# Attention, then an MLP, on one core: another hand-planned order, three split loads, eleven conversions moved off GpSimd

## The chip, the core and the metric

The kernel runs on one core of a Trainium2 chip. Its engines work side by side: TensorE (PE in the profile, PEld for its weight loads), VectorE (DVE), ScalarE (ACT), GpSimd (POOL) and SyncE (SP), which here only issues DMAs. Each engine takes its instructions in the order in which they were put on its queue, and waits at the first one whose inputs are not there. The metric is the device time of one execution in microseconds (us), the median of three runs for the kernel before. A profile is one such execution, recorded instruction by instruction.

## The reference: what is computed

```python
def _attn_ref(q, k, v, g_q, g_k):
    def rmsnorm(x, g):
        rms = np.sqrt(np.mean(x * x, axis=-1, keepdims=True) + 1e-06)
        return x / rms * g
    q_n, k_n = (rmsnorm(q, g_q), rmsnorm(k, g_k))
    scale = 1.0 / np.sqrt(q.shape[-1])
    scores = scale * np.matmul(q_n, k_n.transpose(0, 1, 3, 2))
    attn = softmax(scores)            # row maximum taken off, row sum + 1e-09
    return np.matmul(attn, v)

def _moe_ref(x, w_in, w_out):
    h = x @ w_in
    relu6 = np.clip(h + 3.0, 0.0, 6.0)
    g = h * relu6 / 6.0
    return g @ w_out
```

q, k and v are float32 of shape (batch 8, heads 12, sequence 448, width 64). The attention output, heads side by side, is x with 3584 rows and 768 columns. w_in is 768 x 2048 and w_out 2048 x 768. The result is 3584 x 768 in float32.

## The kernel before

Two heads make a pair; there are six pairs per batch element and 48 in all. A pair's q, k and v are loaded by SP in 256 KB each, with rows spread over 112 partitions and four rows (t = 0 to 3) to a partition. A pair then passes through these steps, named as in the kernel's plan:

- `ld`: a load (line 420). `sq` and `sqh`: squares of q or k, whole or half (L362 on ACT, L364 on POOL). `red2`, `red15`, `redh`: their sums over 64 elements, on DVE (L449, L483). `ln` and `ex`: the inverse root by logarithm and exponential, on ACT (L425, L428). `sc` and `sch`: q or k times it, in bfloat16 (L367; on POOL, a few on DVE).
- `tr` and `trh`: transposes on PE (L537) for the early pairs, with copies `cq`, `ck`, `cqh` out of PSUM (L348 to L358); `dt`: a transposing DMA for the later pairs (L556), after which `kt` multiplies in the gain (L564, L566).
- `s`: scores (L589, L612), two heads at once, each on 64 of PE's rows. `e`: their exponential on ACT (L595, L617). `cv`: v converted to bfloat16 beside a column of ones (L346 on DVE, L348 on ACT, L352 on POOL). `av`, `avh`: exponentials times v, which gives the row sums too (L634, L675). `rd` and `xn`: division by the row sum, on DVE. `xt` and `cx`, or the transposing DMA `dx` (L701): x in transposed form.
- `h1`, `h3`: products with w_in (L748, L767), two steps of three matmuls per group in the main part. `relu` on ACT (L726) and `gate` on DVE (L729) make g. `y384`: products with w_out, 384 columns wide, in four quarter steps of four matmuls (L789). `cy` copies them out, and `st` stores them.
- `w_in` and `w_out`: the weights, in four pieces each, issued by POOL (L820, L825).

The first batch element goes through a stage of its own in two half sequences, so that PE has products with w_in early; the main part then runs attention of one batch element beside the MLP of the one before it. The last 60 us hold MLP work alone.

What sets the order is a plan. All steps are first added to a list by `plan.add`, which numbers them and finds each step's predecessors from what it reads and writes. `Plan.emit` then issues them in the order of the list ORDER, a permutation of the 2386 numbers. `em` ties each instruction to the one issued before it on the same engine, so that ORDER alone decides every engine's order. Steps that more than one engine can do carry a list of engines; the table WAY gives, by number, which is taken, and the first one if the number isn't there:

```python
plan.add("cv", [POOL, ACT, DVE], f_v, [vr], [wr])
...
for i in order:
    kind, engines, fn, preds = self.ops[i]
    fn(engines[WAY.get(i, 0)])
```

A step is named here by its kind and its number: cv589 is step 589, a conversion. The numbers are the same before and after. The functions that the diff touches:

Of the kernel before, what the change touches and what calls it, by code (L numbers as in the profile page):

```python
# [204 lines left out]
def kernel(  # L205
# [11 lines left out]
    nc = tc.nc  # L217
# [4 lines left out]
    NP = B * NPAIR  # L222
# [107 lines left out]
    for t in T_r:  # L330
        nc.vector.memset(t[:, S2:], 0.0)
    for t in eT_r:
        nc.vector.memset(t[:, :, S2:], 0.0)

    NPT = 13
    NXB = 2
    YA = 3
    NSP = 2
    NW0 = 8
    NW1 = 22  # L340

    plan = Plan()
# [65 lines left out]
    def load(P, parts=(0, 1, 2)):  # L408
        b, j = divmod(P, NPAIR)
        hs = slice(2 * j, 2 * j + 2)  # L410
        for i in parts:
            src = (q, k, v)[i]
# [544 lines left out]
```

## Time and profile before

| what | value |
|---|---|
| three runs | 425.29, 425.38 (median), 426.16 us |
| the profiled execution | 425.55 us, of which 423.80 us are the span from first to last instruction |
| granted TensorE clock, mean | 0.998 |
| busy share of the span | PE 98%, ACT 68%, PEld 57%, DVE 53%, POOL 42% |
| DMA | 67.77 MB, mean 160 GB/s |

How to read it: a busy PE is not a PE at its peak, since matmuls overlap and their ends are modelled; the distance from one start to the next tells what one costs. A line of the timeline gives start, length, engine, source line, operation, output<-inputs, and how many were merged; in brackets stands how long the engine was idle before and what ended that. A line of the chain of waits gives start, length and what it was. Groups give a count, the busy time and the mean of one in ns, then the idle time before them and what ended it.

### The profile page before, as it was taken

What the parts mean: (1) busy time and instruction counts of PE and PEld (TensorE: products, weight loads), DVE (VectorE), ACT (ScalarE), POOL (GpSimd) and SP (SyncE); (2) the same over time, 40 slices, a digit from 0 to 9 for tenths busy, and PEclk for the clock granted to TensorE, in tenths of its full rate; (3) what the DMA queues carried; (4) which work ended last, traced back from release to release, by engine and by line L of the source; (5) the groups of instructions that cost most, each with busy time, mean ns of one, the idle gap of its engine ahead of it and who ended that gap; (6) DMA issues with size and microseconds to landing.
All of it is one profiled execution on the core that took longest, in us unless ns stands there. A gap on an engine that the chain in (4) does not pass through costs nothing.

```text
span 423.8 us, 9991 instructions
## 1 busy us (share of the span) xinstructions
PE 414.8 (98%) x3960; PEld 243.0 (57%) x3960; DVE 225.8 (53%) x453; ACT 287.1 (68%) x523; POOL 178.1 (42%) x206
## 2 busy tenths in 40 slices
PE   7999999989999999999999999999999999999996
PEld 3566877645555555555555555555555555555564
DVE  5988774769775476565445455543453433232310
ACT  6999988789987768787767867666846662133101
POOL 3999685678774462593035655333030200000000
PEclk9999999999999999999999999999999999999999
DMA  7999999999869958595768469273144202200323
GB/s 249 292 282 220 244 216 170 274 267 274 207 155 267 249 129 226 172 197 144 198 154 239 110 159 215 79 184 77 40 106 112 57 26 60 43 7 0 109 68 118
DMA packets 98931, 67.77 MB, mean 160 GB/s; under 512 B 53156, under 2 KB 95428, under 8 KB 98884
## 3 DMA queue, kind: packets, MB, share of 16 engines
q1 hardware_dynamic: 93248, 60.50, 54.6%
q0 software_dynamic: 5248, 6.29, 9.0%
q8 instruction: 31, 0.51, 0.5%
q10 hardware_dynamic: 388, 0.34, 0.3%
q14 instruction: 16, 0.13, 0.1%
HBM read 50.23 MB, written 11.01 MB: 145 GB/s over the span
## 4 chain that ended last, share of the span: by engine, by line
PE 84%; DMA 6%; ACT 4%; issue 1%; DVE 1%; SPq 1%; POOL 1%; DVEq 0%; POOLq 0%; ACTq 0%
PE M L767 28%; PE M L789 27%; PE X L675 9%; PE S L589 5%; PE S L789 5%; PE X L589 3%; PE M L748 3%; DMA qk<-in_q_dram 3%; ACT eT L617 3%; DMA w_in_sb<-in_moe_w_in_dram 2%; DMA vf<-in_v_dram 1%; PE X L767 1%; PE S L767 1%; POOL qks L367 1%; PE X L789 1%
## 5 line engine op out<-in xcount | busy, mean ns | idle before, releaser
L367 POOL TENSOR_TENSOR qks<-qk,rs 112x512 bf16<-112x512 f32 (+1 forms) x88 | 88.9, 1024 | 119.5 <-ACT rs L428 94.8
L789 PE MATMUL M<-w_out_sb,gT 128*128 128x384 bf16 x752 | 138.0, 326 | 0.0
L767 PE MATMUL M<-xT,w_in_sb 128*128 128x448 bf16 x618 | 134.0, 353 | 0.0
L789 PEld LDWEIGHTS <-gT 128*128 128x128 bf16 x912 | 84.2, 98 | 58.3 <-issue 7.3
L729 DVE SCALAR_TENSOR_TENSOR gT<-ts,M 128x448 bf16<-128x448 f32 x119 | 73.3, 616 | 74.5 <-ACT ts L726 74.3
L595 ACT ACTIVATE eT<-S 112x896 bf16<-112x896 f32 x112 | 99.7, 916 | 6.9 <-PE X L675 3.6
L726 ACT ACTIVATE ts<-M 128x448 f32<-128x448 f32 x119 | 64.9, 546 | 46.5 <-PE M L767 39.4
L767 PEld LDWEIGHTS <-w_in_sb 128*128 128x128 bf16 x672 | 60.3, 98 | 58.2 <-issue 11.9
L364 POOL TENSOR_TENSOR sq<-qk 112x512 f32<-112x512 f32 (+1 forms) x59 | 59.1, 1012 | 24.1 <-DMA qk<-in_q_dram 9.6
L595 ACT ACTIVATE eT<-X 112x896 bf16<-112x896 f32 x56 | 51.3, 917 | 20.2 <-PE X L589 19.2
L675 PEld LDWEIGHTS <-eT 112*128 112x128 bf16 x1344 | 52.3, 97 | 15.1 <-DVE va L346 1.5
L675 PE MATMUL X<-va,eT 112*128 112x65 bf16 x1344 | 55.3, 193 | 1.4 <-DVE va L346 1.1
L449 DVE TENSOR_REDUCE ssq<-sq 112x16 f32<-112x1024 f32 x42 | 50.7, 1212 | 7.1 <-ACT sq L362 3.8
L589 PE MATMUL S<-T 64*128 64x448 bf16 x224 | 34.1, 353 | 0.1
L350 DVE COPY y<-M 128x384 f32<-128x384 f32 x23 | 12.8, 557 | 39.1 <-PE M L789 39.1
L694 DVE TENSOR_TENSOR xn<-X,rd 112x512 bf16<-112x512 f32 x42 | 28.9, 689 | 2.1 <-DMA xT<-xn 1.3
L691 DVE RECIPROCAL rd<-X 112x8 f32<-112x8 f32 x42 | 8.7, 207 | 38.2 <-PE X L675 35.4
L589 PEld LDWEIGHTS <-T 64*128 64x128 bf16 x336 | 12.3, 94 | 24.0 <-issue 18.8
L362 ACT ACTIVATE sq<-qk 112x512 f32<-112x512 f32 (+1 forms) x38 | 22.2, 595 | 5.6 <-DMA qk<-in_q_dram 3.4
L348 ACT COPY y<-M 128x384 f32<-128x384 f32 x24 | 11.5, 480 | 19.0 <-PE M L789 18.7
L748 PE MATMUL M<-xT,w_in_sb 128*128 128x224 bf16 x192 | 23.1, 259 | 0.2 <-DMA w_in_sb<-in_moe_w_in_dram 0.2
L789 PE MATMUL S<-w_out_sb,gT 128*128 128x384 bf16 (+1 forms) x128 | 22.3, 316 | 0.0
(88 smaller groups left out, 303.1 us busy)
## 6 DMA issues: line engine op xcount, KB each, us to landing
qk<-in_k_dram SPq DMA_DIRECT2D x45, 256.0 KB, 4.2
qk<-in_q_dram SPq DMA_DIRECT2D x45, 256.0 KB, 4.0
vf<-in_v_dram SPq DMA_DIRECT2D x45, 256.0 KB, 4.3
w_in_sb<-in_moe_w_in_dram POOLq DMA_DIRECT2D x4, 768.0 KB, 8.5
w_out_sb<-in_moe_w_out_dram POOLq DMA_DIRECT2D x4, 768.0 KB, 9.2
out_dram<-y SPq DMA_DIRECT2D x7, 336.0 KB, 3.9
out_dram<-y SPq DMA_DIRECT2D x8, 288.0 KB, 3.5
out_dram<-y SPq DMA_DIRECT2D x8, 240.0 KB, 2.7
```

What stands on the lines that cost most here:

```text
L364: em(nc.gpsimd.tensor_tensor(out=out, in0=in_, in1=in_, op=A_MULT))
L367: em((nc.vector if e == DVE else nc.gpsimd).tensor_tensor(out=out, in0=in_, in1=by.unsqueeze(3).to_broadcast(list(in_.shape)), op=A_MULT))
L449: em(nc.vector.tensor_reduce(out=ssq[:].rearrange("p i n -> p (i n)"), in_=sq[:].rearrange("p i (n d) -> p (i n) d", d=D), axis=AX_X, op=A ...
L589: em(nc.tensor.matmul(out=ps[:, a, 0:S], lhsT=qkT[r, S + t * TP:S + t * TP + 128], rhs=qkT[r, 0:S], start=True, stop=True))
L595: em(nc.scalar.activation(out=eT[:, t, 0:S2].rearrange("p (a s) -> p a s", a=2), in_=ps[0:TP, :, 0:S], func=EXP, bias=0.0, scale=1.0))
L675: em(nc.tensor.matmul(out=X_ps[:, a, i * E1:(i + 1) * E1], lhsT=eT[:, t, c:c + 128], rhs=va[:, a, t, :], start=(t == 0 and i == 0), stop=( ...
L694: em(nc.vector.tensor_tensor(out=xn[:].rearrange("p i a d -> p a i d"), in0=view()[:, :, :, 0:D], in1=rd[:].unsqueeze(3).to_broadcast([TP, ...
L726: em(nc.scalar.activation(out=ts[:], in_=ps()[:, 0:S], func=RELU, bias=0.5, scale=1.0 / 6.0))
L729: em(nc.vector.scalar_tensor_tensor(out=out, in0=shape(ts[:]), scalar=1.0, in1=shape(ps()[:, 0:S]), op0=A_MIN, op1=A_MULT))
L748: em(nc.tensor.matmul(out=ps()[:, f * SH:(f + 1) * SH], lhsT=w_in_sb[:, kt, f0:f0 + 128], rhs=xT[:, kt, z * SH:(z + 1) * SH], start=(kt == ...
L767: em(nc.tensor.matmul(out=ps()[:, 0:S], lhsT=w_in_sb[:, kt, f * 128:(f + 1) * 128], rhs=xT[:, kt, :], start=(kt == 0), stop=(kt == NKT - 1)))
L789: em(nc.tensor.matmul(out=ps()[:, 0:nc0], lhsT=gT[:, f, i * 128:(i + 1) * 128], rhs=w_out_sb[:, f, c0:c0 + nc0], start=(f == 0), stop=(f = ...
```

## The change

The kernel after has the same 2386 steps with the same predecessors. Three things differ.

ORDER is another permutation. On PE, the number of instructions of every kind is the same; their sequence differs from the first few microseconds on. The runs of score steps, where PE goes from work on all its rows to work on half of them and back, have 178 edges in place of 180.

WAY has other entries. By kind and engine, before and after: `cv` POOL 26 and 15, DVE 17 and 21, ACT 5 and 12; `sqh` POOL 6 and 4, ACT 6 and 8; `sc` of the first six pairs DVE 4 and 1, POOL 2 and 5; `ck` DVE 9 and 11, ACT 4 and 2; `cq` DVE 5 and 7, ACT 2 and 0; `cqh` DVE 11 and 12, ACT 1 and 0; `cx` DVE 4 and 5, ACT 2 and 1; `kt` DVE 22 and 21, ACT 13 and 14; `cy384` DVE 27 and 29, ACT 28 and 26. `sq`, `sch` and `cxh` keep their numbers per engine.

The loads of v for the last three pairs (NSL = 3) go out as two DMAs of one head each.

```diff
 WAY = {
-    53: 1, 61: 1, 63: 2, 67: 1, 68: 1, 69: 1, 76: 1, 80: 1, 83: 1, 95: 1, 99: 1, 101: 2, 121: 1, 122: 1,
...
+    53: 1, 54: 1, 61: 1, 63: 2, 68: 1, 69: 1, 83: 1, 84: 1, 90: 2, 95: 1, 101: 1, 121: 1, 122: 1, 128: 2,
...
 ORDER = [
-    9, 20, 8, 21, 22, 10, 23, 11, 24, 25, 13, 28, 26, 14, 27, 53, 16, 31, 55, 32, 17, 33, 54, 212, 12, 34,
...
 ]
...
     NPT = 13
     NXB = 2
+    NSL = 3
...
-            def fn(_, dst=dst, src=src, np=np):
+            split = i == 2 and P >= NP - NSL
+
+            def fn(_, dst=dst, src=src, np=np, split=split):
                 rows = src[b, hs].rearrange("h (p t) d -> p h (t d)", t=T)
                 rows = bass.AP(rows.tensor, rows.offset, [[rows.ap[0][0], np]] + [list(d) for d in rows.ap[1:]])
-                em(nc.sync.dma_start(out=dst, in_=rows))
+                for h in ((0, 1) if split else (slice(0, 2),)):
+                    em(nc.sync.dma_start(out=dst[:, h], in_=rows[:, h]))
```

Of the new ORDER, the stretch that matters most for SP reads, loads and transposes alone: dt663, ld262, ld590, ld562, ld561, ld369, ld591, dt760, ld626, ld625, ld396. Before, it was ld262, dt663, ld591, ld532, ld561, ld562, ld625, ld590, dt760, ld626, ld499, ld534, ld746, ld655, ld369.

276 rows, old and new, of tables (ORDER, WAY) are left out of this document.

## The prediction

> **What bounds the kernel now.** I read the page's engine totals, then busy time by stage, then who ends PE's idle time. Engine totals, and stages (columns: stretch, its length, then busy time of PE, PEld, DVE, ACT, POOL, the granted clock, the DMA share, GB/s):
>
> ```profile
> PE 414.8 (98%) x3960; PEld 243.0 (57%) x3960; DVE 225.8 (53%) x453; ACT 287.1 (68%) x523; POOL 178.1 (42%) x206
> ```
>
> ```profile
> 0.00:10.00 10.00, 7.75 (x34) 2.95 (x36) 4.79 (x19) 5.81 (x17) 3.37 (x15) 1.00 0.76 242
> ...
> 10.00:30.00 20.00, 19.03 (x304) 11.82 (x304) 17.96 (x53) 19.84 (x42) 17.78 (x25) 1.00 1.03 285
> 30.00:62.00 32.00, 30.97 (x435) 24.80 (x432) 25.23 (x55) 29.57 (x54) 26.89 (x30) 1.00 1.06 234
> 62.00:100.00 38.00, 36.92 (x421) 23.40 (x420) 24.60 (x45) 31.25 (x59) 25.62 (x27) 1.00 1.07 234
> 100.00:400.00 300.00, 300.00 (x2642) 167.04 (x2639) 149.77 (x279) 198.42 (x350) 104.49 (x112) 1.00 0.55 138
> ...
> 400.00:423.80 23.80, 20.08 (x140) 12.94 (x137) 3.51 (x7) 2.24 (x5) 0.00 (x0) 0.97 0.29 84
> ```
>
> From 100 to 400 us PE shows no idle time, so another order can gain there only by making the matmuls themselves cost less; it can lose without limit. What there is to win stands in four places: 2.25 us before 10 us, 0.97 in 10 to 30, 1.03 in 30 to 62, 1.08 in 62 to 100. In 10 to 30 ACT is full (19.84 of 20), with DVE and POOL close behind; later every engine but PE has room. The 1.08 us is one wait:
>
> ```profile
> 82.44 0.47 SPq L420 DMA_DIRECT2D vf<-in_v_dram  x1
> ...
> 88.86 0.69 DVE L346 TENSOR_SCALAR_CACHE_REDUCE va<-vf 112x512 bf16<-112x512 f32 x1 [2.35 <-DMA vf<-in_v_dram]
> 89.59 0.69 DVE L346 TENSOR_SCALAR_CACHE_REDUCE va<-vf 112x512 bf16<-112x512 f32 x1
> 89.61 1.15 PE L675 MATMUL X<-va,eT 112*128 112x65 bf16 x32 [1.08 <-DVE va L346]
> 89.64 1.04 POOL L364 TENSOR_TENSOR sq<-qk 112x512 f32<-112x512 f32 x1 [2.44 <-DVE va L346]
> ```
>
> The value load ld369 leaves SP at 82.44, its conversion cv589 starts 6.42 us later, and the attention product av762 waits. The chain of waits tells why the load left so late: two scalings on POOL hold the transpose dt760, and SP's next loads stand behind that.
>
> ```profile
> 75.98 2.06 POOL qks L367 x2
> 78.03 0.02 issue
> 78.05 1.23 SPq L556
> ...
> 82.44 6.31 DMA vf<-in_v_dram
> ```
>
> The profiled run took 425.55 us: 423.80 of span and 1.75 around it; the three runs' median is 425.38. I sum against 425.55 and take 0.17 off at the end. A change under 0.2% (0.85 us) can't be told from none: the band is 424.53 to 426.23.
>
> **PE's fixed work.** Matmuls overlap, so their recorded 326 or 353 ns are not what PE pays; starts that follow each other tell it.
>
> ```profile
> 83.56 0.81 PE L789 MATMUL M<-w_out_sb,gT 128*128 128x384 bf16 x4
> 84.31 0.55 PE L589 MATMUL S<-T 64*128 64x448 bf16 x4
> 84.70 0.35 PE L589 MATMUL X<-T 64*128 64x448 bf16 x2
> 84.98 2.12 PE L789 MATMUL M<-w_out_sb,gT 128*128 128x384 bf16 x12
> 87.04 0.36 PE L589 MATMUL X<-T 64*128 64x448 bf16 x2
> ...
> 87.71 0.82 PE L789 MATMUL M<-w_out_sb,gT 128*128 128x384 bf16 x4
> ```
>
> Twelve L789 take 87.04 - 84.98 = 2.06 less an edge, so 0.163 each and 0.65 for a step of four. Two score pairs take 0.39 (84.31 to 84.70), so 0.195 a pair; but the last pair before other work takes 0.28 (84.70 to 84.98), and the four L789 before the scores 0.75, not 0.65. So going into a run of scores and coming out of it costs about 0.1 us each. ORDER has 180 such edges before and 178 after: **-0.2 us**. The instructions on PE are the same in number and kind.
>
> **The start, up to step av516.** In both orders the same 161 plan steps of PE lie up to av516 (near 42.1 us in this execution), so the other engines can be compared by counting. ACT gains sqh54, sqh84, sqh230 and sqh248, cv101 and cxh358, and loses sqh214, sqh232, cqh67, ck80 and cxh199.
>
> ```profile
> 42.16 1.08 PE X L675 x32
> ...
> 67.76 1.30 PE M L789 x8
> ...
> 95.11 0.97 PE X L675 x32
> ```
>
> These are from the chain of waits: av516 and its three fellows, y453 and the step after it, and four av steps, 0.24 us each. ACT's own:
>
> ```profile
> 8.24 0.40 ACT L362 ACTIVATE sq<-qk 112x256 f32<-112x256 f32 x1
> ...
> 8.69 0.35 ACT L348 COPY gT<-M 128x224 bf16<-128x224 bf16 x1
> ...
> 10.97 0.62 ACT L356 ACTIVATE gT<-M,gp_t 128x448 bf16<-128x448 bf16 x1
> ```
>
> ```profile
> L348 ACT CAST va<-vf 112x512 bf16<-112x512 f32 x5 | 3.1, 625 | 0.0
> ```
>
> Two half squares more (0.80), one conversion (0.62), a half copy in for a half copy out (0), a half copy (0.35) and a ck (0.62) out: +0.45 us, and ACT has 0.16 us of idle time in 10 to 30 to put it in. I take +0.4 at av516. Up to y453, the first y step (67.76 us here), the two lists agree again: after trades cx523 and ck608 for ck515, cq542, cx552 and a square for e660, each a few tenths, and what was gained goes back. I keep **+0.1 us** there, since ACT is full only in the first part. Ends: -0.6, if the 1.03 us of PE idle time in 30 to 62 halves, and +1.6, from POOL:
>
> ```profile
> L367 POOL TENSOR_TENSOR qks<-qk,rs 112x512 bf16<-112x512 f32 (+1 forms) x88 | 88.9, 1024 | 119.5 <-ACT rs L428 94.8 <-DMA T<-qks 14.9 <-issue 7.1
> L352 POOL CAST va<-vf 112x512 bf16<-112x512 f32 x23 | 13.9, 613 | 12.4 <-PE X L675 12.1 <-POOL qks L367 0.2
> ```
>
> POOL gains sc76, sc99 and sc126 from DVE (3 x 1.02), two half squares (2 x 0.61), cv346 (0.61) and sq525 (as a scaling, 1.02), and loses four half squares and three conversions (7 x 0.61): +1.6 us. POOL is idle 2.22 us in 10 to 30 (17.78 of 20), which covers it; if its waits don't move, it comes out at w_in1, the second piece of the first weights, which POOL issues at 31.57 and the chain of waits has on it for 8.44 us.
>
> ```profile
> 31.57 8.44 DMA w_in_sb<-in_moe_w_in_dram
> ```
>
> A rule speaks about these moves. Beside the scaling sc99 on DVE, the short scaling sch100 on POOL, 0.61 us alone, took longer: three POOL instructions of 0.61, 1.02 and 0.61 filled 2.81 us, 0.57 too much.
>
> ```profile
> 8.99 0.61 POOL L367 TENSOR_TENSOR qks<-qk,rs 112x256 bf16<-112x256 f32 x1
> ...
> 12.23 2.81 POOL L367 TENSOR_TENSOR qks<-qk,rs 112x256 bf16<-112x256 f32 x3
> ...
> 13.87 0.69 DVE L367 TENSOR_TENSOR qks<-qk,rs 112x512 bf16<-112x512 f32 x1
> ```
>
> The Trainium skill (SBUF — State Buffer, Who interferes with whom) says that a DVE instruction with two SBUF inputs and a GpSimd instruction that reads SBUF exclude each other, and that the tensor_scalar form which writes its accumulator doesn't take the shared ports; the trace agrees with both (the 0.57 us here; 1.04 us for the POOL square at 89.64 beside a conversion on DVE). By that rule three clashes go, up to 3 x 0.57 = 1.7 us comes back on POOL: its end of +1.6 would be about 0 and the POOL rival below would fall, with the sum as it is. The same skill (Perfetto Trace Analysis, Optimizing Scalar/DVE Operations) warns that moving work between GpSimd and DVE might not help because of that port; the 1.04 us says that the form used here pays nothing.
>
> **The wait at 89.61.** After has SP's order dt663, ld262, ld590, ld562, ld561, ld369, ld591, dt760: ld369 is ahead of dt760 and seven loads earlier. From ld369 to av762 ORDER now holds 8.9 us of PE work (5.6 before), counted with the steps above. Even the old 6.42 and 0.69 for the conversion, 7.1, fit: **-1.25 us** (1.08 of recorded idle, 1.25 by the starts: 87.71 + 0.65 = 88.36 to 89.61). Two things take its place.
>
> First, cv589 stays on DVE and now stands ahead of cx672, the copy that score s752 needs. From ld369 to s752 lie 5.2 us of PE work: five quarter y steps (3.25), three score pairs and two edges (0.77), four av (0.97) and a transpose step (0.2). Against that stand the landing, 0.69, and 0.39 for cx672:
>
> ```profile
> 77.90 0.39 DVE L350 COPY xT<-X 128x448 bf16<-128x448 bf16 x1 [0.68 <-PE X L710]
> ```
>
> The landing lies between 3.25 (a load two places behind a transpose, from 74.75 to the square that waited for it at 78.00) and 6.42 (ld369 itself, twelfth):
>
> ```profile
> 74.75 0.99 SPq L420 DMA_DIRECT2D qk<-in_q_dram  x2
> 78.00 0.63 ACT L362 ACTIVATE sq<-qk 112x512 f32<-112x512 f32 x1 [1.53 <-DMA qk<-in_q_dram]
> ```
>
> By place in the burst, fifth between second and twelfth, it is 3.25 + 0.3 x 3.17 = 4.2, as is the median of all value loads:
>
> ```profile
> vf<-in_v_dram SPq DMA_DIRECT2D x45, 256.0 KB, 4.3
> ```
>
> So 4.2 + 0.69 + 0.39 - 5.2 = **+0.1 us**, ends 0 and 2.3. Second, ld262 moves behind dt663, and its cv560 from POOL to DVE: 4.2 us of PE work to av665 against 3.25 to 6.42 and 0.69. As the first load behind a transpose I take the low end: 3.94, covered; ends 0 and 2.9, **+0.1 us**. ACT's sq770 waits for the third load of the burst with 3.4 us of PE work; a wait of about 1 us there is hidden, since the next score needs ACT's e757 only 2 us after its end.
>
> **The rest.** GpSimd keeps 15 of 26 conversions; DVE has 21 instead of 17, ACT 12 instead of 5. Beyond 100 us that is at most 4.4 us more on ACT and 3.1 on DVE (4 x 0.69, and reading the accumulator), over 300 us in which ACT is idle 102 and DVE 150: 0. If one of them stands ahead of a copy that PE waits for, it costs its wait, 0 to 1.25. The last three value loads go out in two halves: three more issues of 0.47 us on SP, where PE is never idle, so 0 both ways; without that cover they delay a load by 0.5. No PE step reads half a tile, so nothing starts sooner.
>
> **Sum:** 425.55 - 0.2 + 0.1 - 1.25 + 0.1 + 0.1 = 424.40; less 0.17 for the median: **424.2 us**.
>
> **Rivals.** *The stall comes back at av665 (slower).* ld262 and its conversion on DVE stand behind dt663, and if they fare as ld369 did, av665 waits 6.42 + 0.69 - 4.2 = 2.9 us: 424.2 - 0.1 + 2.9 = 427.0 (and s752, which follows, finds its own data there). It starts to cost above a landing of 3.5 us and makes the kernel slower than before above 4.8. For it: eleven loads and two transposes leave SP within 7.4 us of PE work. Against: the place in the burst. 0.17.
> *POOL binds the start (slower).* The 1.6 us come out at w_in1, and by y453 POOL has another square ahead (1.0): 424.2 + 2.6 - 0.1 = 426.7. For it: 17.78 of 20 busy. Against: idle time and clashes that go. 0.13.
> *A late conversion blocks DVE or ACT (slower by little):* one wait such as the old one, 424.2 + 1.25 = 425.5. 0.10.
> *The order does nothing:* the load lands late again, and the start pays what was won: 425.4. 0.07.
> *The start gets shorter too:* its -0.6 instead of +0.1, and no wait in the burst: 424.2 - 0.7 - 0.2 = 423.3. 0.13.
>
> **How the numbers follow.** The forecast, 0.40, has its own range 423.8 to 425.2; 0.27 of it lies under 424.53, 0.13 in the band. Faster: 0.27 + 0.13 = 0.40; same: 0.13 + 0.10 + 0.07 = 0.30; slower: 0.17 + 0.13 = 0.30. Leaving out a tenth at either end, the range is 423.4 to 427.0; its upper end adds part of a second wait to the POOL case.
>
> **What would show it.** PE idle ended by DVE va gone near 89 us; DVE's wait for vf short, and no wait for a score behind the copy at L350 near 83 us; av516 at 42.4 to 42.6; PE busy 300 of 300 from 100 to 400 us. Wrong it would be if a second engine held PE for over a microsecond before 100 us, or if any idle time of PE showed after it.

## The result, and the profile after

The changed kernel takes 423.75 us (median of 22 executions, 422.46 to 427.52), the kernel before 425.78 (22 executions in the same set, 423.86 to 427.79): a ratio of 0.9958, 95% interval 0.9944 to 0.9972, or 1.8 us less. (The ratio isn't the quotient of the two medians, which lie 2.0 us apart.) A second set, run later, gave 0.9946 (0.9933 to 0.9959). It is faster by about 0.5%, near the 424.2 us that was forecast and just under 423.8 us, where the forecast's own range began. But most of the gain lies where the forecast had none.

The profiled execution of the changed kernel took 424.52 us, with a span of 422.4. Its busy time by stage (columns as in the prediction):

```profile
0.00:10.00 10.00, 7.91 (x35) 3.25 (x35) 4.65 (x20) 5.87 (x17) 3.23 (x15) 1.00 0.79 243
10.00:30.00 20.00, 18.97 (x318) 12.57 (x315) 18.23 (x55) 19.94 (x43) 19.79 (x27) 1.00 1.05 289
30.00:62.00 32.00, 30.69 (x431) 25.03 (x428) 24.77 (x56) 28.71 (x54) 25.79 (x29) 1.00 1.08 237
62.00:100.00 38.00, 37.95 (x416) 22.97 (x414) 26.74 (x51) 29.40 (x55) 25.82 (x27) 1.00 1.05 220
100.00:400.00 300.00, 299.40 (x2637) 167.79 (x2637) 154.19 (x282) 200.77 (x355) 98.35 (x102) 1.00 0.57 138
```

From 62 to 100 us PE's idle time has gone from 1.08 to 0.05 us, as forecast; from 100 to 400 us, where it had none, it now has 0.60. ACT is still full from 10 to 30 us, and POOL has joined it (19.79 of 20, from 17.78). The timeline of the changed kernel at the two places where the forecast looked for the wait and for what would take its place (SP, DVE and PE):

```profile
76.49 0.47 SPq L425 DMA_DIRECT2D vf<-in_v_dram  x1
...
77.41 0.69 DVE L348 TENSOR_SCALAR_CACHE_REDUCE va<-vf 112x512 bf16<-112x512 f32 x1 [1.48 <-DMA vf<-in_v_dram]
...
81.62 0.69 DVE L348 TENSOR_SCALAR_CACHE_REDUCE va<-vf 112x512 bf16<-112x512 f32 x1
...
82.23 0.39 DVE L352 COPY xT<-X 128x448 bf16<-128x448 bf16 x1
82.67 0.36 PE L594 MATMUL X<-T 64*128 64x448 bf16 x2
```

ld369 leaves at 76.49 and cv589 runs at 81.62 without a wait of DVE. cx672 stands behind it, and the score step s752 starts when cx672 is done; the PE work ahead of it ended 0.17 us earlier, of which 0.10 is the edge of a run of scores. Farther on, at 100 us, stands a new wait:

```profile
99.16 0.68 DVE L571 TENSOR_SCALAR_CACHE_REDUCE T<-T,gp_t 128x448 bf16<-128x448 bf16 x1 [0.77 <-DMA T<-qks]
...
99.77 0.62 DVE L734 SCALAR_TENSOR_TENSOR gT<-ts,M 128x448 bf16<-128x448 f32 x1
...
100.44 0.73 PE L772 MATMUL M<-xT,w_in_sb 128*128 128x448 bf16 x3 [0.44 <-DVE gT L734]
```

The key scaling kt845 waits 0.77 us for its transposing DMA, the gate gate684 stands behind it on DVE, and PE waits for the gate: 0.60 us by the starts.

### The profile page after: what moved, and what is told of

The parts are those of the page before. It is cut to its first block, busy times and chain, and to the rows that moved or that the text cites. A ratio compares the mean times of both kernels' runs of the same rounds, so it can differ in the third digit from the quotient of the medians.

```text
span 422.4 us, 9979 instructions
## 1 busy us (share of the span) xinstructions
PE 414.2 (98%) x3959; PEld 244.1 (58%) x3960; DVE 230.6 (55%) x464; ACT 287.6 (68%) x525; POOL 173.0 (41%) x196
## 3 DMA queue, kind: packets, MB, share of 16 engines
q0 software_dynamic: 5248, 6.29, 9.1%
## 4 chain that ended last, share of the span: by engine, by line
PE 82%; DMA 7%; ACT 6%; SPq 2%; DVE 1%; POOL 1%; issue 1%; POOLq 0%; DVEq 0%
PE M L772 27%; PE M L794 26%; PE X L680 9%; PE S L594 5%; PE S L794 5%; PE M L753 4%; ACT eT L622 4%; PE X L594 3%; DMA w_in_sb<-in_moe_w_in_dram 2%; DMA T<-qks 2%; DMA qk<-in_k_dram 2%; SPq L425 1%; PE X L772 1%; DMA qk<-in_q_dram 1%; PE S L772 1%; ACT sq L364 1%
## 5 line engine op out<-in xcount | busy, mean ns | idle before, releaser
L369 POOL TENSOR_TENSOR qks<-qk,rs 112x512 bf16<-112x512 f32 (+1 forms) x91 | 91.2, 1021 | 106.5 <-ACT rs L433 77.5
L600 ACT ACTIVATE eT<-S 112x896 bf16<-112x896 f32 x112 | 100.4, 916 | 16.3 <-PE S L594 9.1
L731 ACT ACTIVATE ts<-M 128x448 f32<-128x448 f32 x119 | 64.8, 545 | 42.6 <-PE M L772 28.8
L366 POOL TENSOR_TENSOR sq<-qk 112x512 f32<-112x512 f32 (+1 forms) x57 | 58.1, 1026 | 49.7 <-DMA qk<-in_q_dram 31.5
L352 DVE COPY y<-M 128x384 f32<-128x384 f32 x26 | 14.5, 557 | 31.0 <-PE M L794 30.9
L350 ACT COPY y<-M 128x384 f32<-128x384 f32 x21 | 10.0, 478 | 19.5 <-PE M L794 19.4
```

Source lines behind the costliest of these rows:

```text
L366: em(nc.gpsimd.tensor_tensor(out=out, in0=in_, in1=in_, op=A_MULT))
L369: em((nc.vector if e == DVE else nc.gpsimd).tensor_tensor(out=out, in0=in_, in1=by.unsqueeze(3).to_broadcast(list(in_.shape)), op=A_MULT))
L600: em(nc.scalar.activation(out=eT[:, t, 0:S2].rearrange("p (a s) -> p a s", a=2), in_=ps[0:TP, :, 0:S], func=EXP, bias=0.0, scale=1.0))
L731: em(nc.scalar.activation(out=ts[:], in_=ps()[:, 0:S], func=RELU, bias=0.5, scale=1.0 / 6.0))
```

## One number per stage: how far PE is behind its own work

Two profiles of one kernel differ by about a microsecond. At 20 us that goes with when the first loads land: the q load of step 13 landed at 9.1 and 9.0 us in the changed kernel's profile and in f2's, at 8.4 us in f1's and e8's, and the delays in the table below are 3.71, 3.75, 2.96 and 2.94 us. So the runs below are compared by PE's delay: the start of a PE step less the sum of what the PE steps ahead of it take when nothing holds them (each kind's usual distance between starts, and 0.1 us for each edge of a run of scores). It is worked out from all PE rows of a profile, here at 20, 60 and 100 us of such work and in its last 10 us (400). "Early" is the stretch from the exponential of step 103 to that of step 157, near 10 and 15 us on ACT. What follows PE's last row isn't in the table: 3.9 us to the end of the span before, 3.4 us after, in the recorded pair.

| kernel | start | early | 20 | 60 | 100 | 400 | 60 to 100 | 100 to 400 |
|---|---|---|---|---|---|---|---|---|
| before | before | 6.00 | 4.16 | 5.90 | 7.60 | 9.13 | 1.70 | 1.53 |
| e1 load 369 early | before | 6.29 | 4.40 | 6.95 | 7.89 | 9.42 | 0.94 | 1.53 |
| e6 ck80 on DVE | before | 6.08 | 4.38 | 6.46 | 8.68 | 10.20 | 2.22 | 1.52 |
| e3 rest changed | before | 6.23 | 4.02 | 7.48 | 10.32 | 12.17 | 2.84 | 1.85 |
| changed | changed | 5.50 | 3.71 | 5.35 | 6.62 | 8.51 | 1.27 | 1.89 |
| changed, again (f1) | changed | 5.51 | 2.96 | 4.76 | 6.68 | 8.56 | 1.92 | 1.88 |
| e4 loads whole | changed | 5.52 | 3.28 | 4.15 | 6.26 | 8.15 | 2.11 | 1.89 |
| e2 start changed | changed | 5.52 | 3.41 | 4.93 | 6.52 | 8.05 | 1.59 | 1.53 |
| e8 e2 and load 369 | changed | 5.51 | 2.94 | 4.08 | 5.86 | 7.39 | 1.78 | 1.53 |
| f4 e8 and weights | changed | 5.52 | 3.19 | 4.54 | 5.39 | 6.92 | 0.85 | 1.53 |
| e7 pairs exchanged | changed | 5.49 | 3.21 | 4.10 | 5.48 | 7.23 | 1.38 | 1.75 |
| f2 e7 and weights | changed | 5.51 | 3.75 | 5.27 | 5.79 | 7.55 | 0.52 | 1.76 |
| e5 first 21 us changed | mixed | 5.50 | 3.49 | 5.34 | 6.92 | 8.45 | 1.58 | 1.53 |

At 60 us the four kernels with the start before are 5.90 to 7.48 behind, mean 6.70; the eight with the changed start 4.08 to 5.35, mean 4.65: 2.0 us (1.8 without e3, which holds a drop of the clock told of below). The recorded profiles of before and after are the best of the one kind and the worst of the other: 0.55 apart. (f3, whose start is neither, is left out.) The row of the first products with w_out (PE groups of the tile; the times are those of the first and last start) shows the same for e1 and e7:

```profile
L769 PE MATMUL M<-w_out_sb,gT x48: 323/326/337, 68.6 to 79.2; 128*128 128x384 bf16 x48
```

```profile
L772 PE MATMUL M<-w_out_sb,gT x56: 322/326/337, 66.4 to 80.0; 128*128 128x384 bf16 x56
```

One wait between 20 and 60 us is common to nearly all of them. PE's step 283 is the first that needs w_in1, the second piece of the first weights, which POOL issues. In eleven of the thirteen profiles (not in e3 and e5) it starts 0.05 us after that piece has landed. From the chains of waits, before and then after:

```profile
31.57 8.44 DMA w_in_sb<-in_moe_w_in_dram
...
40.05 0.75 PE M L748 x6
```

```profile
30.80 9.11 DMA w_in_sb<-in_moe_w_in_dram
...
39.96 0.75 PE M L753 x6
```

The four kernels with the start before issue it at 31.57 to 32.66 us (mean 32.2), the eight with the changed start at 29.82 to 30.84 (mean 30.3); it lands at 40.6 and at 39.0 us on average. In the recorded pair the issue is 0.77 us sooner but the landing only 0.10, and PE loses 0.94 us there after, 0.40 before. So that pair is nearly level again there. No run moves this issue alone, so how much of the start's gain it carries isn't shown.

## Experiments

All ratios are to the kernel before, timed in the same set on the same chip.

**e1: the wait of av762 alone.** The kernel before, one step moved in ORDER:

```diff
-644, 465, 645, 760, 737, 661, 754,
+644, 465, 645, 369, 760, 737, 661, 754,
```

> The kernel before with one move: the value load ld369 stands directly ahead of the transpose dt760 in ORDER, instead of seven places behind it. Theory (the wait of av762 is what the change takes away): ld369 leaves SP near 77.5 us, cv589 doesn't wait, the PE wait of 1.08 us near 89.6 us is gone, and the time falls by 1.0 to 1.3 us, a ratio of 0.997. Rival (the gain lies in the start, or in the order of the scores): the wait goes, but the time falls by less than 0.4 us. Rival (the wait moves on): another DMA is late in its place, PE waits for it, ratio 1.000.

Measured: 424.70 us, ratio 0.9989 (0.9973 to 1.0006), so about 0.5 us, perhaps nothing. In its profile DVE no longer waits for vf before cv589, and PE no longer waits at av762. But the delay from 60 to 100 us falls by 0.76, not 1.25: PE now waits 0.29 us near 96 us for a gate behind a key scaling that waits for its DMA, and 0.21 near 88.7. DVE of e1 near 96 us:

```profile
94.95 0.68 DVE L546 TENSOR_SCALAR_CACHE_REDUCE T<-T,gp_t 128x448 bf16<-128x448 bf16 x1 [0.58 <-DMA T<-qks]
...
95.56 0.62 DVE L709 SCALAR_TENSOR_TENSOR gT<-ts,M 128x448 bf16<-128x448 f32 x1
```

Here a PE that comes 1.25 us sooner finds the next DMA late.

**e2 and e3: the change cut in two** at step 453, the first product with w_out (67.6 us).

```diff
 # e2: ORDER and WAY of after up to 453, then the steps left, in the order before
 # e3: ORDER and WAY of before up to 453, then the steps left, in the order after
```

> ORDER and WAY of after up to step y453 (near 67.7 us), then the remaining steps in the order and on the engines of before. Theory: the two starts end level, so this is the kernel before, within 0.4 us, and the wait at av762 is there again; ratio 0.999 to 1.001. Rival (the start carries the gain): 1.5 us or more faster, ratio 0.996.

> ORDER and WAY of before up to step y453, then the remaining steps as in after, with the split loads. Theory: nearly the whole gain, 1.3 to 2 us, ratio 0.9955 to 0.997. Rival (the start carries the gain): within 0.5 us of before, ratio 0.999 to 1.001.

Measured: e2 423.19 us, ratio 0.9959 (0.9946 to 0.9971); e3 426.94 us, 1.0044 (1.0028 to 1.0060). The start alone carries the whole gain, with the old wait still there (0.76 us at av762 in e2's profile). The rest behind the old start is slower: near 70 us PE loses 0.68, 0.56 and 0.86 us to copies and a division on DVE, most of which the changed start has done ahead of time. (Some executions of e3 also show a drop of PE's clock, told of at the end; the five without it take 426.35 us on average, still more than the kernel before.) So the two halves aren't worth separate amounts that add up.

**e4: the split loads whole again.**

```diff
-    NSL = 3
+    NSL = 0
```

> After with the last three value loads in one piece each again (NSL = 0). Theory: PE doesn't wait there, so it is as fast as after: ratio to before 0.994 to 0.997. Rival (the halves matter): 0.4 us or more of the gain is lost, ratio 0.997 or above.

Measured: 424.01 us, ratio 0.9977 (0.9963 to 0.9992). By the marks set ahead of the run that is the rival's side: up to 0.8 us lost. But the interval overlaps that of the changed kernel's first set (0.9944 to 0.9972) and not that of its second (0.9933 to 0.9959), the sets aren't all from one chip, and no row of e4 shows a wait for an unsplit load: from 100 to 400 us it loses 1.89, as the changed kernel does. What the split is worth stays open. What the profile did show is another thing: the DVE order that cost 0.07 us above, the edge taken off, costs 1.08 us of idle time here, because the same load landed late.

```profile
81.46 0.69 DVE L348 TENSOR_SCALAR_CACHE_REDUCE va<-vf 112x512 bf16<-112x512 f32 x1 [1.14 <-DMA vf<-in_v_dram]
...
82.07 0.39 DVE L352 COPY xT<-X 128x448 bf16<-128x448 bf16 x1
...
82.51 0.37 PE L594 MATMUL X<-T 64*128 64x448 bf16 x2 [1.08 <-DVE xT L352]
```

**e5 and e6: what in the start.** e5 keeps the changed order only up to step 200 (21 us); e6 is the kernel before with the key copy 80 on DVE.

```diff
 # e5: ORDER and WAY of after up to 200, then the steps left, in the order before
 # e6: WAY of before, without the entry
-    80: 1,
```

> The changed kernel's order and engines up to the scores step 200 (at about 21 us), the order before from there on; the last loads are whole. Theory ScalarE: up to 20 us ScalarE is the bound (19.84 and 19.94 us busy of 20 between 10 and 30 us), the change takes the copy of a key piece (L358, 0.63 us on ScalarE) from between its second and third exponential of head scores, and that is where the start gains: the three profiles with the start before show TensorE 4.02 to 4.40 us behind its work at 20 us, the three with the changed start 3.28 to 3.71. Then this kernel has some 3.5 us there, and its time is 0.6 to 0.8 us below that of the kernel before (ratio 0.998 to 0.9985). Rival (the gain is made between 40 and 68 us, where the start before loses 0.5 to 0.7 us at waits for exponentials and the changed one 0.2): within 0.2 us of the kernel before, or slower, since the order before finds other steps done than it was made for.

> The kernel before with one engine choice changed: the key copy of step 80 (L358) goes from ScalarE to VectorE; no step is moved in the order. Theory ScalarE: the distance of the exponentials' starts from step 103 to step 157 falls from 6.0 us to about 5.5, and the time by 0.4 to 0.6 us (ratio 0.9986 to 0.999). Rival (what the start gains lies in the whole order, so that the next late operation takes the place of this one): the distance stays at 5.8 us or more, and the time moves by less than 0.2 us.

Measured: e5 424.17 us, ratio 0.9977 (0.9965 to 0.9989): the first 21 us give 1.0 us, about half of the gain (what gives the rest of the start's gain, made between 21 and 60 us, no run separates). e6 425.68 us, 1.0010 (0.9995 to 1.0024): nothing. ACT between the exponentials 103 and 157, first in the kernel before, then in the changed kernel, then in e6:

```profile
9.87 0.90 ACT L617 ACTIVATE eT<-S 112x896 bf16<-112x896 f32 x1
...
10.97 0.62 ACT L356 ACTIVATE gT<-M,gp_t 128x448 bf16<-128x448 bf16 x1
...
11.85 0.90 ACT L617 ACTIVATE eT<-S 112x896 bf16<-112x896 f32 x1
...
14.63 1.24 ACT L362 ACTIVATE sq<-qk 112x256 f32<-112x256 f32 x3
...
15.87 0.92 ACT L617 ACTIVATE eT<-S 112x896 bf16<-112x896 f32 x1
```

```profile
10.06 0.90 ACT L622 ACTIVATE eT<-S 112x896 bf16<-112x896 f32 x1
...
11.37 0.90 ACT L622 ACTIVATE eT<-S 112x896 bf16<-112x896 f32 x1
12.16 0.93 ACT L364 ACTIVATE sq<-qk 112x256 f32<-112x256 f32 x2
12.99 0.20 ACT L430 ACTIVATE rs<-ssq 112x12 f32<-112x12 f32 x1
...
13.34 1.71 ACT L622 ACTIVATE eT<-S 112x896 bf16<-112x896 f32 x2
...
15.04 0.63 ACT L364 ACTIVATE sq<-gT 112x512 f32<-112x512 f32 x1
15.55 0.92 ACT L622 ACTIVATE eT<-S 112x896 bf16<-112x896 f32 x1
```

```profile
10.01 0.90 ACT L596 ACTIVATE eT<-S 112x896 bf16<-112x896 f32 x1
...
11.57 0.90 ACT L596 ACTIVATE eT<-S 112x896 bf16<-112x896 f32 x1
12.94 0.21 ACT L404 ACTIVATE rs<-ssq 112x12 f32<-112x12 f32 x1 [0.48 <-DVE ssq L462]
...
14.85 1.23 ACT L341 ACTIVATE sq<-qk 112x256 f32<-112x256 f32 x3
...
16.09 0.92 ACT L596 ACTIVATE eT<-S 112x896 bf16<-112x896 f32 x1
```

With the copy gone ACT waits 0.48 us for row sums that DVE now delivers later, and three squares still stand in front of exponential 157. The changed order has two squares in that wait (12.16) and one in front of 157 (15.04).

**f3: those two moves together, in the kernel before.**

```diff
-    80: 1,            # WAY
-... 63, 97, 88, ... 216, 122, 114, 121, 133, ...
+... 63, 122, 121, 97, 88, ... 216, 114, 133, ...
```

> The kernel before with two edits in its first 16 us: the key copy of step 80 goes to VectorE, as in the run that did this alone, and the squares of steps 122 and 121 (0.42 and 0.63 us on ScalarE) go ahead of the logarithm of step 97, into the wait that ScalarE had there. Theory (these two are what the changed start does between the exponentials 103 and 157; with the copy gone alone ScalarE only waited longer, 0.48 us, for the row sums behind step 97): the distance from step 103 to step 157 falls from 6.0 to 6.3 us to 5.3 to 5.6 us, and the time by 0.4 to 0.8 us, ratio 0.998 to 0.999. Rival (the rest of the order before is not ready for earlier exponentials and the gain is lost before 40 us): the distance falls and the ratio is 0.9995 or more.

Measured: 428.25 us, ratio 1.0052 (1.0035 to 1.0069), 2.2 us slower. The early stretch took 7.99 us. The order before loads an input of these squares later than the changed one (its q at 7.3 against 4.8 us), and ACT stood at it; DVE and PE waited behind. All six executions also have a mean clock of 0.990 to 0.996, so part of the 2.2 us is the drop of the clock told of at the end. One row each of ACT and PE:

```profile
13.34 0.94 ACT L341 ACTIVATE sq<-qk 112x256 f32<-112x256 f32 x2 [1.31 <-DMA qk<-in_q_dram]
```

```profile
16.42 0.36 PE L516 MATMUL M<-identity,qks 112*128 112x112 bf16 x4 [1.98 <-DVE gT L337]
```

So neither the copy alone nor the copy with the two squares is what the start gains. That loads, squares and engines have to change together is argued from this, not shown; which least set does it wasn't found.

**e7, e8, f2, f4: what is left past 60 us.** e7 exchanges three pairs of neighbours in the changed kernel; e8 is e2 with ld369 ahead of dt760; f2 and f4 are e7 and e8 with the last two weight loads issued sooner.

```diff
 # e7, in ORDER of after (moved steps; the rest as it was)
-655, 589, 796, ... 654, 672, 755      -816, 845, 794 ... 880, 684, 817     -1192, 1358, 1187, 1386
+655, 796, ... 654, 672, 589, 755      +816, 684, 845, 794 ... 880, 817     +1192, 1187, 1386, 1358
 # f2 and f4, beside e7's and e8's moves
-417, 5, 418 ... 439, 6, 605 ... 603, 7, 630
+417, 5, 6, 7, 418 ... 439, 605 ... 603, 630
```

> The changed kernel with three pairs of neighbours exchanged: the value conversion 589 behind the copy 672 on VectorE, the gate 684 ahead of the key scaling 845 on VectorE, the scores step 1358 behind the scores step 1386 on TensorE. Theory (what TensorE still waits past 60 us can be had back one by one, since nothing else is late there): the waits of 0.17 (1.25 in the profile with whole loads), 0.60 and 0.33 us go, the profile shows TensorE busy for 299.8 or more of the 300 us from 100 to 400 us, and the time is 0.9 to 1.6 us below that of the changed kernel: a ratio of 0.992 to 0.9937 to the kernel before. Rival (each wait passes to the next operation behind it): 0.9950 to 0.9965, as the changed kernel.

> The changed start up to step 453 and the order before from there, as in the run with the changed start, and in it the value load 369 moved directly ahead of the transposes 760 on SyncE's queue. Theory (the wait of TensorE for the conversion 589 at 88 us, 0.76 us in the profile with the changed start, costs what it shows): the wait is gone and the time is 0.6 to 1.0 us below that of the changed start alone, a ratio of 0.9935 to 0.9945 to the kernel before. Rival (as the same move made in the kernel before: the wait goes in the profile and the time moves by a third of it or less, since other waits come for it): 0.995 to 0.9965.

Measured: e7 423.62 us, ratio 0.9959 (0.9947 to 0.9971); e8 423.55 us, 0.9964 (0.9952 to 0.9976). Both are no better than the kernel that they mend. In e8 and e7 the waits aimed at are gone (e7 has 0.19 us of idle time left from 100 to 400 us), but e7 loses 0.39 us at the next score step near 100 us, which now waits for a division on DVE, and at 73 us both have a wait that the lists of waits of before and after don't show: PE has caught up with the last weights. The changed kernel is already at that limit: its last weights land at 73.8 us, and their first use starts at 73.85, 0.17 us late. The rows of e8:

```profile
73.49 0.81 PE L767 MATMUL M<-w_out_sb,gT 128*128 128x384 bf16 x4 [0.88 <-DMA w_out_sb<-in_moe_w_out_dram]
```

```profile
L803 POOL DMA_DIRECT2D w_out_sb<-in_moe_w_out_dram x4: 740/803/815, 52.4 to 61.5; - x4
...
DMA to landing us min/median/max: 8.8/9.9/11.9
```

> The changed kernel once more, beside the three kernels of this call, so that they can be set against it on one chip. Expected: 0.9944 to 0.9972 of the kernel before, as measured.

> The changed kernel with the three exchanged pairs, and in it the issues of the last two output-weight loads (steps 6 and 7, at 59.7 and 61.6 us) moved on GpSimd directly behind the one of step 5 at 54.4 us, into 1.6 us in which GpSimd was idle. Theory A (the landing of the last weight load near 73 us is set by its issue, and it is what takes back the gain made ahead of it: waits of 0.40 to 0.88 us in the three quickest profiles): no wait for it is left, and the time is 0.4 to 0.9 us below that of the exchanged pairs alone, ratio 0.9935 to 0.995. Theory B (the DMA engines are full up to 70 us, shares of 1.0 to 1.16, so the loads only share the same stretch and the last one lands as late): the wait stays, ratio 0.9950 to 0.9968.

> The changed start up to step 453, the order before from there with the value load 369 ahead of the transposes 760, and the last two output-weight loads issued behind the one of step 5, as in the run with the exchanged pairs. Theory A (the issue sets the landing): the wait of 0.88 us at 73 us that the same kernel showed without this edit goes, ratio 0.9935 to 0.995. Theory B (the DMA engines are full): it stays, ratio 0.9955 to 0.997.

Measured in one set: f1 423.23 us, 0.9946 (0.9933 to 0.9959); f2 423.34 us, 0.9948 (0.9935 to 0.9962); f4 422.80 us, 0.9934 (0.9920 to 0.9948). The first and last issue of the four loads (POOL, us), the times to their landing, and PE at 73 us, in f4:

```profile
L803 POOL DMA_DIRECT2D w_out_sb<-in_moe_w_out_dram x4: 742/756/817, 52.4 to 55.4; - x4
...
DMA to landing us min/median/max: 8.1/11.8/16.3
```

```profile
73.00 1.31 PE L767 MATMUL M<-w_out_sb,gT 128*128 128x384 bf16 x7
```

In f4 the last load is issued at 55.4 in place of e8's 61.5 us, and the wait is gone. But the load lands only about 1.7 us sooner (55.4 + 16.3 against 61.5 + 11.9): the DMA engines are as full as before, and both theories hold in part. f2 can't tell them apart. Its last load lands at 72.7 us, e7's at 72.9, and PE, 1.2 us farther behind at 60 us than in e7, comes for it only at 73.6. From e8 to f4 the ratio, each to the kernel before of its own set, falls by 0.003 (1.3 us), and f4 is the quickest kernel of all by its median; against f1 in the same set it is 0.4 us, within the intervals. f2 stays as quick as f1, although its profile is 1.0 us less behind at the end (7.55 against 8.56). Why the exchanges show in the profiles and not in the times is open. The profiled executions of the changed kernel, 424.52 and 424.43 us, are slower than its medians, those of e7 and f2 (423.08, 423.31) are not; whether the waits for DMAs that the exchanges remove are shorter without the profiler wasn't tried.

## Why the prediction was near, and for which of its steps that is right

*The start, +0.1 (ends -0.6 and +1.6): wrong in sign and size.* It counted ACT's instructions up to av516, found 0.45 us more, and put them on the path. Yet with that work added, the way from exponential 103 to 157 got shorter: 5.49 to 5.52 us in nine profiles with the changed order there, 6.00 to 6.29 in the four with the order before; and f3, where it took 7.99, is slower. That these exponentials, and what stands between them, hold PE in the first 20 us is argued from this; e6 and f3, which were to show it, didn't shorten the way. In the recorded pair av516 came at 42.0 against 42.1 us, not at 42.4 to 42.6; over all profiles the start gains about 1.8 to 2.0 us by 60 us. The rival "the start gets shorter too" had the direction; its price (-0.6) was a third of it, and it looked for it from 30 to 62 us, while e5 makes about half of the gain in the first 21. The feared end, POOL, had the right path and the wrong sign: POOL's busy time from 10 to 30 us rose by 2.01 us for the 1.6 counted, but this filled idle time, and w_in1, at which the cost was to come out, was issued 0.77 us sooner in the recorded pair and 1.9 us sooner on average.

The rule weighed there (the Trainium skill, SBUF — State Buffer, Who interferes with whom) was to give up to 1.7 us back, three times the clash seen at 13.87 us. But that one was the only clash of the three: there the scaling on POOL took 1.06 in place of 0.61 us, while at the other two DVE scalings (9.47 and 18.27 us) POOL was ending an instruction of its usual 0.61 us or stood idle. So 0.45 us came back.

*The wait at av762, -1.25: the wait went, its worth didn't come.* In the profile it is gone as forecast, at the place and by the load named. Alone it was worth 0.5 us (e1, 0.3 lost to 1.1 gained), and from 60 to 100 us the changed kernel loses 1.27, 1.92 and 2.11 us in three profiles, the kernel before 1.70: nothing gained that the spread would show. It went to the next term in e4 and f1 (1.15 and 0.87), and in all three to the gate near 100 us (0.40 to 0.61).

*cx672 behind cv589, +0.1 (0 to 2.3): inside its ends, too low.* With the edge taken off, 0.07 us in the profile after, 1.15 and 0.87 in the two other profiles of this order (e4 and f1). The landing was taken as 4.2 us by place in the burst; in e4, where DVE waited for it, cv589 started 6.2 us after its load, near the high end of 6.42.

*av665, +0.1, and its rival at 427.0: right that it costs nothing.* DVE waited 1.48 us for the load, cv560 ended at 78.10, and av665 ran at 79.4 without a wait.

*Edges, -0.2: nothing speaks against it.* The PE work summed over the two orders differs by 0.19 us, but that sum uses the same price of an edge, and 0.2 us can't be told in the times.

*The rest, 0 (to 1.25): too low.* Past 100 us the changed order loses 1.89, 1.88 and 1.89 us in its three profiles; the order before loses 1.52 or 1.53 in seven. So 0.36 us more, of which 0.23 stand at one scores step near 177 us that waits for a division on DVE (0.33 by the starts, with its edge). The 0.6 us of gate684 stand just before the 100 us mark of this count. That no idle time of PE would show past 100 us was given as a mark of being wrong, and it showed.

*The sum.* About -1.8 for the start, 0 from 60 to 100 us, +0.36 behind, -0.19 for the edges make -1.6, beside the measured -1.8. The forecast had +0.1, -1.05, 0 and -0.2, which is -1.15. That the total came near is luck: a gain of about 1 us that didn't come was made up for by one of nearly 2 us that the forecast didn't have.

## What to carry to other kernels

Where an engine is full in a stage, don't count its instructions up to a milestone: take the chain of operations that the next engine waits for, measure the distance between two of them, and ask what stands in between. A wait seen in one profile is worth at most the distance to the next thing that is late, which here was often another DMA behind it; cut the change in two and run the halves before pricing it. And take several profiles before a stage is called faster or slower: here one and the same start differed by over a microsecond from profile to profile, and the first pair hid a gain of nearly two.

## What was not expected of the hardware

Drops of PE's clock followed short waits. In e3 two waits of 0.66 and 0.61 us within two microseconds, in f3 one of 1.98 us and, 20 us later, two of 0.58 and 0.61, were each followed by a granted clock of 0.50 for 3.4 us. PE's timeline around e3's two waits, and then e3 by the microsecond (columns as before, the granted clock the third from the end):

```profile
32.77 0.37 PE L520 MATMUL S<-identity,qks 112*128 112x112 bf16 x4 [0.66 <-POOL qks L347]
...
34.67 0.56 PE L520 MATMUL S<-identity,qks 112*128 112x112 bf16 x4 [0.61 <-POOL qks L347]
```

```profile
33.00:34.00 1.00, 0.94 (x23) 0.70 (x20) 0.76 (x4) 0.95 (x3) 0.98 (x2) 1.00 0.51 174
34.00:35.00 1.00, 0.39 (x6) 0.34 (x5) 0.52 (x2) 0.91 (x2) 1.00 (x2) 0.83 0.82 128
35.00:36.00 1.00, 1.00 (x10) 0.86 (x8) 0.45 (x1) 0.53 (x2) 1.00 (x2) 0.50 1.03 153
...
37.00:38.00 1.00, 1.00 (x12) 0.89 (x10) 0.57 (x2) 0.79 (x1) 0.98 (x2) 0.50 1.24 206
38.00:39.00 1.00, 1.00 (x19) 0.71 (x18) 0.94 (x1) 0.72 (x2) 1.00 (x2) 0.97 1.20 203
```

Of e3's nine executions the four with a mean clock of 0.996 took 427.45 us on average, the five at 1.00 took 426.35: the drop, with the waits that came before it, costs about 1.1 us. The longest executions of before and after (428.09 and 427.52 us) have that mean clock too. The Trainium skill (TensorE: Matmul & The Clock Gate, Why this matters for your kernels) asks for no idle gaps over about 3 us, since a window of idle halves the clock; the half clock agrees with the 0.50 here, the length of gap doesn't: gaps of 0.66 and 0.61 us came before it. Short waits alone aren't the cause, though. Single ones of 1.08 us (before at 89.61, e4 at 82.51, e6 at 90.69), and in e3 itself three of 0.61, 0.48 and 0.78 us from 70 to 73 us, where PE was busy for 1.13 of 3 us, were followed by no drop. What else it takes is open.
